# Moving the bulk weight loads of a fused adaLN, sliding-attention and MLP kernel to the GpSimd queue

## The chip, the cores and the metric

One core of one Trainium2 chip. The metric is the device time of one execution in microseconds (us); for the kernel before it is the median of 7 runs, 181.19 us (178.92 to 184.17). The profiled execution is one of these, at 178.92 us, and its span from first to last instruction is 177.2 us, so 1.7 us lie around the span. Sums are made inside the span.

## The reference

A transformer block with modulated layer norms: D = 448, 2048 tokens, 16 heads of 28, an attention in which each token sees 8 earlier tokens at a distance of 2, and an MLP with F = 1792. All tensors are bf16.

```
mod = silu(c) @ w_mod                      # six rows of 448: sa, ca, ga, sb, cb, gb
h = layernorm(x) * (1 + ca) + sa
q, k, v = split(h @ wqkv)                  # 16 heads of 28
o = softmax over the 8 keys at s, s-2, ..., s-14 (those >= 0) of (q . k) / sqrt(28), times v
x = x + ga * (o @ wo)
h = layernorm(x) * (1 + cb) + sb
x = x + gb * (gelu(layernorm(h) @ w1 + b1) @ w2 + b2)
```

## The kernel before

**Tiles and stages.** The tokens are split by parity into two sequences of 1024, so that a distance of 2 becomes a distance of 1, and into 16 blocks of 128 tokens. There are five kinds of work:

- the head: loads of x, of the first modulation columns (`wm_st`), of the Q, K, V weights; silu(c) and two groups of small matmuls give the scale and shift columns `mod_col`;
- `front_ln` and `front_qk` for chunks of 2, 2, 4, 4 and 4 blocks: statistics (L505, L506), 1/std, normalized rows z (L528), a transpose into hT, then the matmuls `pq` (Q and K, L585 and L591) and `pv` (V). The first 8 blocks are transposed on TensorE (L639); the other 8 by DMA transposes (L657) with scale and shift applied afterwards on VectorE (L661). V rows are cast into `vstage` and stored to the HBM scratch `v_hbm` (L719);
- `attention(b)`, nine of them: V windows loaded back from `v_hbm` into `vb` (L782), scores `lt` (L796), exponentials (L806), mask (L814), denominators `pd` (L828), products `po` (L836), division into `oT` (L862);
- `out_proj(t)`, 16 of them: `pw` (L877), residual (L881), the second and third layer norm with 1/std on GpSimd (L523), rows y (L528), a DMA transpose into yT (L903), the residual with bias `x1p` on GpSimd (L907);
- `mlp(j)`, four tiles of 512 tokens: w1 matmuls (`p<-yT,w_s`, L585 and L591), gelu (L937), w2 matmuls (`p<-w_s,hm`, L950), sum (L958), store.

Three phases follow each other: attention 0 to 4 and MLP tile 0; attention 5 and 6 and tile 1; attention 7 and 8 and tiles 2 and 3. The work up to the first w1 matmul is here called the front part.

**What sets the order.** Each piece is a task with an engine, an assumed time and the keys that it reads and writes. A list scheduler (`Planner.forward`, L148) simulates the engines with these assumed times, tries 300 orders by changing ranks (`plan`, L243), and emits every engine's instructions in the order of the best one. Engines run in that order and wait by semaphores alone. An entry of `order_after` places a task in the planned order, but makes no semaphore wait.

**Queues.** In the kernel before every DMA but one is issued from SyncE, in order: the head loads, then (marked `free`, so that the planner may place them anywhere) the second modulation weights `wmod2`, `wo_s`, x blocks 8 to 15, the biases, `w1_s`, `w2_s`, and between them the V stores (L719), the V window loads (L782), the transposes and the outputs. Each DMA takes the next of 8 completion semaphores, and waits until the DMA eight before it has landed. `mods()` (L724) makes four broadcast modulation rows: matmul `pb` (L731), a cast on ScalarE, a store to `mod_hbm` (L738), a broadcast load `mod_bc` (L740), with which `wo_s` (L743) and `w2_s` (L758) are scaled on VectorE.

**Weights of Q and K.** They land in `wqk_st` in two halves of the contraction rows each (`wq` a and b, `wk` a and b). `spread` (L666, instruction L675) copies them so that a head of 28 takes 32 columns: one copy for each half of the rows, four in all. In VectorE's order the four are q a, k a, q b, k b. Every `pq` of Q needs both q copies.

Of the kernel before, what the change touches and what calls it, by code (L numbers as in the profile page):

```python
# [11 lines left out]
FP32 = mybir.dt.float32  # L12
# [5 lines left out]
DP = 512  # L18
KT = 4
KOFF = (0, 128, 192, 320)  # L20
HP = 32
FT = F // 128
# [25 lines left out]
DMA_RATE = 330e3  # L48
SWITCH, SAME = 0.095, 1.0
SEM = 0.07  # L50
DRAIN = {"PE": 0.165, "DVE": 0.085, "ACT": 0.105, "POOL": 0.05, "SP": 0.0}
# [27 lines left out]
class Planner:  # L79
# [68 lines left out]
    def forward(self):  # L148
# [13 lines left out]
        while len(order) < len(self.tasks):  # L162
            started = False
            for e in ("PE", "DVE", "ACT", "POOL", "SP"):
# [4 lines left out]
                for t in ready[e]:  # L169
                    if ready_at[t] > now or (shared and t.port):  # L170
                        continue
                    key = (t.rank + (SAME if e == "PE" and t.mode_in == mode else 0.0), -t.n)
                    if best is not None and key < best_key:
                        continue
                    need = {}
                    for b in t.bufs:
                        if b.slot is None:
                            need[b.room] = need.get(b.room, 0) + 1
                    if all(sum(x <= now for x in room[r]) >= n for r, n in need.items()):
                        best, best_key = t, key  # L180
# [99 lines left out]
def kernel(  # L280
# [57 lines left out]
    mod_col = cst.tile([128, 2 * KT], FP32, name="mod_col")  # L338
    mod_half = cst.tile([128, 2 * KT], FP32, name="mod_half")
# [29 lines left out]
    chain_dma = []  # L369

    def load(fn, nbytes, writes, reads=(), bufs=(), free=False):
        t = add("SP", max(0.5, nbytes / DMA_RATE), fn, writes=writes, reads=reads, bufs=bufs, late=1.8,
                order_after=list(chain_dma))
        if not free:
            chain_dma[:] = [t]

    def load_k(dst, src, key, bufs=(), free=False):
        n = src.shape[1]
        for h in range(2):
            load(lambda h=h: nc.sync.dma_start(out=dst()[:, 2 * h:2 * h + 2],  # L380
                                               in_=src[KOFF[2 * h]:KOFF[2 * h] + 256].rearrange("(kt p) n -> p kt n", p=128)),
                 256 * n * 2, [key + "ab"[h]], bufs=bufs, free=free)

    def load_m(dst, col, key, bufs, free=False):
        src = w_mod[:, col:col + 2 * D]
        load(lambda: nc.sync.dma_start(out=dst()[:, 0:2], in_=src[0:256].rearrange("(kt p) n -> p kt n", p=128)),
             512 * D * 2, [key + "a"], bufs=bufs, free=free)
        load(lambda: nc.sync.dma_start(out=dst()[:, 3], in_=src[320:448]), 256 * D * 2, [key + "b"], bufs=bufs, free=free)
        load(lambda: nc.sync.dma_start(out=dst()[64:128, 2], in_=src[256:320]), 128 * D * 2, [key + "c"], bufs=bufs, free=free)

    def fill_m(dst, key, bufs, one, rank):

        def fn():
            nc.gpsimd.memset(dst()[0:64, 2], 0.0)
            if one is not None:
                nc.gpsimd.memset(dst()[0:1, 2, one:one + D], 1.0)

        add("POOL", 1.3, fn, writes=[key + "z"], bufs=bufs, rank_add=rank)

    def load_x(b0, b1):  # L400
        load(lambda: nc.sync.dma_start(out=x_all[:, b0:b1, :], in_=xv[b0 // 8, :, b0 % 8:(b1 - 1) % 8 + 1, :]),
             (b1 - b0) * 128 * D * 2, [f"x{b}" for b in range(b0, b1)], free=b0 >= 8)
# [3 lines left out]
    add("ACT", 0.4, lambda: nc.scalar.dma_start(out=c_row[:], in_=c), writes=["c_row"], late=1.6, rank_add=500)  # L406

    tbl0 = add("ACT", 1.28, lambda: nc.scalar.preload_act_table_set(EXP_SET), rank_add=400)
    load_x(0, 2)
    fill_m(lambda: wm_st.t[:], "wm", [wm_st], D, 850)  # L410
    load_m(lambda: wm_st.t[:], 0, "wm", [wm_st])
    load_k(lambda: wqk_st.t[:, 0], A_wqkv[:, 0:D + HP - DH], "wq", [wqk_st])
    load_k(lambda: wqk_st.t[:, 1], A_wqkv[:, D:2 * D + HP - DH], "wk", [wqk_st])
    load_x(2, 4)
    load_k(lambda: Wv[:], A_wqkv[:, 2 * D:3 * D], "wv")
    load_x(4, 8)
# [7 lines left out]
    load(v_pads, 3 * LEAD * DP * 2, ["v_pads"], reads=["warm_w"], free=True)  # L424
    for i in range(2):
        fill_m(lambda i=i: wmod2[i].t[:], f"wmod2{i}", [wmod2[i]], 0 if i == 1 else None, 300)
        load_m(lambda i=i: wmod2[i].t[:], (2 + 2 * i) * D, f"wmod2{i}", [wmod2[i]], free=True)
    add("POOL", 1.6, lambda: nc.gpsimd.memset(wo_s[:], 0.0), writes=["wo"], rank_add=440)
    wo_v = A_wo.rearrange("(ft r d) n -> r d ft n", r=4, d=DH)
    for r in range(4):  # L430
        load(lambda r=r: nc.sync.dma_start(out=wo_s[HP * r:HP * r + DH, :, :], in_=wo_v[r]), D * D // 2, [f"wo{r}"],
             reads=["wo"], free=True)
    for b in (8, 12):
        load_x(b, b + 4)
    b2_bc = sb("zh", [128, D], BF16, "b2_bc")
    load(lambda: nc.sync.dma_start(out=b2_bc.t[:], in_=B_b2.partition_broadcast(128)), 128 * D * 2, ["b2"], bufs=[b2_bc], free=True)
    load(lambda: nc.sync.dma_start(out=b1_rows[:], in_=B_b1.rearrange("(f p) -> f p", p=128)), F * 2, ["b1_rows"], free=True)
    for kt in range(KT):
        load(lambda kt=kt: nc.sync.dma_start(out=w1_s[:, kt], in_=B_w1[KOFF[kt]:KOFF[kt] + 128]), F * 256, [f"w1{kt}"], free=True)
    for i in range(4):  # L440
        f0, f1 = 4 * i, min(4 * i + 4, FT)
        load(lambda f0=f0, f1=f1: nc.sync.dma_start(
            out=w2_s[:, f0:f1], in_=B_w2[128 * f0:128 * f1].rearrange("(ft p) n -> p ft n", p=128)),
            (f1 - f0) * 256 * D, [f"w2l{f // 2}" for f in range(f0, f1, 2)], free=True)
# [8 lines left out]
    late_pool = []  # L453

    def pool_late():
        gate = add("POOL", 0.1, lambda: nc.gpsimd.memset(wqk_st.t[0:1, :, KT - 1, 0:8], 0.0), bufs=[wqk_st],
                   writes=["wqb", "wkb"])
        for us, fn, writes, reads, ra in late_pool:
            add("POOL", us, fn, writes=writes, reads=reads, rank_add=ra, order_after=[gate])

# [4 lines left out]
         ["ident"], gated=False, rank_add=800)  # L465
    pool(0.1, lambda: nc.gpsimd.memset(neg_half[:], -0.5), ["neg_half"])
# [72 lines left out]
    def c_cols():  # L539
        for kt in range(KT):  # L540
            nc.tensor.matmul(psc.t[:, kt:kt + 1], lhsT=c_row[0:1, KOFF[kt]:KOFF[kt] + 128], rhs=one1[:],
                             start=True, stop=True)

    P.wrote(add("PE", 0.2, c_cols, mode="32x128", reads=["c_row", "one1"], bufs=[psc]), psc)
    add("ACT", 0.15, lambda: nc.scalar.activation(out=e_c[:], in_=psc.t[:], func=ACT.Exp, scale=-1.0), bufs=[psc],
        writes=["e_c"], after=[tbl0])
    add("DVE", 0.08, lambda: nc.vector.tensor_copy(out=c_col[:], in_=psc.t[:]), bufs=[psc], writes=["c_col"])
    add("DVE", 0.08, lambda: nc.vector.tensor_scalar_add(out=e_c[:], in0=e_c[:], scalar1=1.0), writes=["e_c"])
    add("DVE", 0.1, lambda: nc.vector.reciprocal(out=e_c[:], in_=e_c[:]), writes=["e_c"])

    def silu():
        nc.vector.tensor_tensor(out=silu_bf[:], in0=e_c[:], in1=c_col[:], op=ALU.mult)
        nc.vector.memset(silu_bf[0:64, 2:3], 0.0)
        nc.vector.memset(silu_bf[0:1, 2:3], 1.0)

    add("DVE", 0.2, silu, reads=["e_c", "c_col"], writes=["silu"])
    pscol = ps_one([128, 2 * KT], "ps_col")

# [482 lines left out]
```

The softmax here doesn't subtract the row's maximum and nothing guards it: scores larger than these inputs give would overflow.

## Time and profile before

| | |
|---|---|
| median of 7 runs | 181.19 us |
| profiled execution, and its span | 178.92 us, 177.2 us |
| TensorE busy in the span | 165.5 us (93%) |
| VectorE, ScalarE, GpSimd busy | 117.0, 107.6, 49.9 us |
| first Q matmul; last `pw` before the MLP ends; first w1 matmul | 9.30; 67.78; 70.79 us |
| last w2 sum starts; end of span | 174.26; 177.2 us |
| bytes moved by DMA | 19.84 MB, nearly all on the queue of SyncE |
| one DMA issue on SyncE | 0.34 to 0.6 us; a DMA transpose 1.25 us |
| the one DMA issue on ScalarE (c) | 0.50 us |

TensorE appears as PE, its weight loads as PEld, VectorE as DVE, ScalarE as ACT, GpSimd as POOL, SyncE as SP; "SPq" is a queue's issue. A line number is that of the listing above. In the waits and the timelines, the engine after the arrow is the one whose work ended the wait.

### The profile page before, as it was taken

How to read it: one execution, taken by the hardware profiler on the slowest of the kernel's cores; microseconds unless marked ns; L12 is line 12 of the kernel's file. 1: busy time of each engine (PE TensorE's matmuls, PEld its weight loads, DVE VectorE, ACT ScalarE, POOL GpSimd, SP SyncE). 2: the span in 40 equal slices, each digit the busy share in tenths (PEclk: the TensorE clock that was granted, in tenths of full speed). 3: DMA queues.
4: the chain of work that ended last, by engine and by line, in shares of the span. 5: the costliest groups of instructions: out<-in, count | busy, mean ns of one | idle time of the engine just before them, and what ended most of it. 6: DMA issues, size and time to landing. Idle time of an engine off the chain costs nothing.

```text
span 177.2 us, 5017 instructions
## 1 busy us (share of the span) xinstructions
PE 165.5 (93%) x2067; PEld 79.9 (45%) x2085; DVE 117.0 (66%) x318; ACT 107.6 (61%) x195; POOL 49.9 (28%) x83
## 2 busy tenths in 40 slices
PE   7898999979999993999999999999999999999993
PEld 2554644444445431434555343555444354443562
DVE  2768995657999789999148459995589962010121
ACT  3347959887884977555838975825975520725200
POOL 8460022001125517754022036342053442000000
PEclk9999999999999999999999999999999999999999
DMA  5999945576997995201401600026100114001011
GB/s 167 321 357 308 281 122 120 147 170 111 318 268 192 321 141 144 66 2 28 95 4 34 191 0 4 1 58 117 55 4 0 31 30 111 0 4 52 0 52 52
DMA packets 28725, 19.84 MB, mean 112 GB/s; under 512 B 14465, under 2 KB 28062, under 8 KB 28702
## 3 DMA queue, kind: packets, MB, share of 16 engines
q1 hardware_dynamic: 28700, 19.52, 42.0%
q8 instruction: 16, 0.26, 0.6%
q14 instruction: 7, 0.06, 0.1%
q10 hardware_dynamic: 2, 0.00, 0.0%
HBM read 12.41 MB, written 3.96 MB: 92 GB/s over the span
## 4 chain that ended last, share of the span: by engine, by line
PE 74%; DMA 11%; DVE 4%; SPq 3%; ACT 3%; issue 2%; ACTq 0%
PE p L950 25%; PE p L585 21%; PE pw L877 6%; PE pq L585 6%; PE p L591 5%; DMA v_hbm<-vstage 4%; PE pv L585 3%; DMA x_all<-in_A_x_dram 3%; DMA yT<-y 2%; PE lt L796 2%; DMA vb<-v_hbm 2%; PE po L836 2%; DVE st_all L505 2%; PE pq L591 2%; SPq L380 1%
## 5 line engine op out<-in xcount | busy, mean ns | idle before, releaser
L937 ACT ACTIVATE hm<-p,b_col 128x512 bf16<-128x512 f32 x56 | 34.9, 687 | 30.1 <-PE p L585 16.1
L950 PE MATMUL p<-w_s,hm 128*128 128x448 bf16 (+1 forms) x238 | 44.8, 342 | 0.0
L585 PE MATMUL p<-yT,w_s 128*128 128x512 bf16 x160 | 38.7, 380 | 3.8 <-issue 3.5
L523 POOL TENSOR_TENSOR rs_all<-tv_all,neg_half 128x1 f32<-128x1 f32 (+1 forms) x34 | 22.6, 673 | 55.2 <-DVE tv_all L520 50.8
L950 PEld LDWEIGHTS <-hm 128*128 128x128 bf16 x238 | 22.4, 98 | 18.9 <-issue 0.9
L958 DVE TENSOR_TENSOR x_all<-p,x1p 128x448 bf16<-128x448 f32 (+1 forms) x17 | 10.1, 596 | 29.8 <-PE p L950 29.8
L907 POOL TENSOR_TENSOR x1p<-x_all,gbb_bc 128x448 f32<-128x448 bf16 x16 | 17.7, 1108 | 33.8 <-DVE x_all L958 12.9
L585 PEld LDWEIGHTS <-w_s 128*128 128x128 bf16 x168 | 15.2, 98 | 23.7 <-issue 7.8
L585 PE MATMUL pq<-hT,Wqk 128*128 128x512 bf16 (+1 forms) x111 | 23.0, 334 | 1.2 <-issue 0.6
L806 ACT ACTIVATE et<-lt 128x464 bf16<-128x464 f32 x36 | 17.3, 571 | 8.3 <-PE lt L796 8.2
L505 DVE BATCH_NORM_STATS2 st_all<-x_all 128x6 f32<-128x448 bf16 x32 | 19.0, 613 | 2.6 <-DMA x_all<-in_A_x_dram 2.5
L814 DVE TENSOR_TENSOR et<-et,mask 128x928 bf16<-128x928 bf16 x18 | 11.7, 667 | 6.0 <-ACT et L806 6.0
L528 DVE TENSOR_SCALAR z<-x_all,mv,rs_all 128x512 bf16<-128x512 bf16 (+1 forms) x32 | 13.0, 426 | 3.7 <-POOL rs_all L523 1.8
L585 PEld LDWEIGHTS <-Wqk 128*128 128x128 bf16 x120 | 10.4, 98 | 10.2 <-issue 2.5
L877 PE MATMUL pw<-wo_s,oT 128*128 128x448 bf16 x64 | 14.5, 354 | 0.3 <-DVE oT L862 0.2
L881 DVE TENSOR_TENSOR x_all<-pw,x_all 128x448 bf16<-128x448 f32 x16 | 9.9, 617 | 5.5 <-PE pw L877 5.5
L862 DVE TENSOR_TENSOR oT<-po,den 128x456 bf16<-128x456 f32 x18 | 10.7, 626 | 3.7 <-ACT den L852 3.7
L701 ACT CAST qT<-pq 128x512 bf16<-128x512 f32 (+1 forms) x20 | 9.3, 512 | 5.2 <-PE pq L591 3.2
L585 PE MATMUL pv<-Wv,hT 128*128 128x448 bf16 x48 | 10.4, 353 | 0.0
L715 ACT CAST vstage<-pv 128x448 bf16<-128x448 f32 x16 | 7.9, 554 | 4.2 <-PE pv L591 3.8
L701 ACT CAST kT<-pq 128x512 bf16<-128x512 f32 (+1 forms) x20 | 9.1, 512 | 2.1 <-PE pq L585 1.3
L849 ACT ACTIVATE den<-pd 128x464 f32<-128x464 f32 x18 | 9.2, 572 | 1.4 <-PE pd L828 1.4
(85 smaller groups left out, 172.4 us busy)
## 6 DMA issues: line engine op xcount, KB each, us to landing
w_s<-in_B_w_dram SPq DMA_DIRECT2D x7, 448.0 KB, 4.7
vb<-v_hbm SPq DMA_DIRECT2D x18, 128.0 KB, 2.8
v_hbm<-vstage SPq DMA_DIRECT2D x8, 256.0 KB
out_dram<-x_all SPq DMA_DIRECT2D x7, 224.0 KB, 3.0
x_all<-in_A_x_dram SPq DMA_DIRECT2D x3, 448.0 KB, 6.2
wqk_st<-in_A_wqkv_dram SPq DMA_DIRECT2D x4, 226.0 KB
wmod<-in_w_mod_dram SPq DMA_DIRECT2D x2, 448.0 KB
x_all<-in_A_x_dram SPq DMA_DIRECT2D x2, 224.0 KB
```

The costliest lines, as they stand in the source:

```text
L505: add("DVE", 0.53, lambda: nc.vector.bn_stats(out=st_all[:, sl, :], in_=src()), reads=key, writes=[f"st{sl}"])
L523: lambda: nc.gpsimd.tensor_tensor(out=rs_all[:, which, b0:b0 + n], in0=tv_all[:, which, b0:b0 + n], in1=neg_half[:, 0:n], op=ALU.pow),
L528: return add("DVE", us, lambda: nc.vector.tensor_scalar(out=dst(), in0=src(), scalar1=mv[:, b, 0:1], scalar2=rs_all[:, which, b:b + 1], op ...
L585: nc.tensor.matmul(outs[i].t[:], lhsT=w(i, kt, slice(0, 128)), rhs=x(i, kt, slice(0, 128)), start=(n == 0 and not last), stop=(n == 2 and ...
L591: nc.tensor.matmul(outs[i].t[:], lhsT=w(i, kt, rows), rhs=x(i, kt, rows), start=not last, stop=last, tile_position=(r0, 0))
L701: add("ACT", 0.06 + n / 1200, lambda dst=dst, p=pq[i]: nc.scalar.copy(out=dst, in_=p.t[:]), bufs=[pq[i]], writes=w)
L806: ex = add("ACT", 0.45, lambda r=r: nc.scalar.activation(out=et.t[:, r].rearrange("p n ft c -> p (n ft c)"), in_=lts[r].t[:].rearrange("p ...
L814: nc.vector.tensor_tensor(out=ev, in0=ev, in1=mask[:], op=ALU.mult)
L877: nc.tensor.matmul(pw.t[:], lhsT=oT[:, ft, c0:c0 + 128], rhs=wo_s[:, ft, :], start=(ft == 0), stop=(ft == 3))
L907: P.wrote(add("POOL", 1.05, lambda: nc.gpsimd.tensor_tensor(out=xp.t[:], in0=x_all[:, t, :], in1=gbb2_bc[:], op=ALU.add), reads=[f"x{t}", ...
L937: gl = add("ACT", 0.57, lambda f=f, p=p1[i]: nc.scalar.activation(out=hm_at(f), in_=p.t[:], func=ACT.Gelu_apprx_tanh, bias=b1_col[:, f:f + ...
L950: nc.tensor.matmul(p2.t[:], lhsT=hm_at(f)[:, bi * 128:(bi + 1) * 128], rhs=w2_s[:, f, c0:c1], start=(f == 0), stop=(f == FT - 1))
```

## The change

1. **Bulk loads go to GpSimd.** `wmod2` (4 DMAs), `wo_s` (4), x blocks 8 to 15 (2), b2 (1), `w1_s` (4) and `w2_s` (4) are issued from GpSimd's queue, in this order, after a gate that waits for the last copy of `spread`.
2. **Each is held back.** Ahead of each bulk DMA (of `wo_s` only the first) VectorE writes one element of its target; the DMA waits for that write. In the planner the write stands after the bulk load two before it; on the chip that is only a place in VectorE's order.
3. **Stores move.** The V rows and the modulation rows are stored from ScalarE's queue. SyncE keeps the head loads, V windows, `mod_bc`, transposes and outputs: 66 DMAs where it had 97.
4. **Q and K are spread by head halves**: a copy takes all rows of 8 heads, so it needs both halves of its weight, and a `pq` needs one copy. VectorE's order is q 0, q 1, k 0, k 1.
5. **The modulation weights** lie on 112 partitions of 4 rows each, loaded in two DMAs of 448 KB that need no zero fill; the constant 1 comes from an addend (`one_cb`, `tensor_scalar_add`) in place of a row of ones.
6. **The planner** knows a DMA bandwidth resource "BW" beside the issue time (0.8 us for a bulk DMA on GpSimd, 0.5 us on ScalarE).

```
-DMA_RATE = 330e3
+DMA_RATE, TR_BYTES = 340e3, 400e3
...
+    def bulk(fn, nbytes, writes, at, reads=(), bufs=()):
+        k = len(chain["bulk"])
+        if at is not None:
+            add("DVE", 0.06, lambda: nc.vector.memset(at(), 0.0), writes=[f"go{k}"], bufs=bufs, order_after=chain["bulk"][-2:-1])
+        t, u = dma("POOL", 0.8, fn, nbytes, writes, list(reads) + [f"go{k}"], bufs, chain["bulk_t"], 2.2)
+        chain["bulk_t"] = [t]
...
+    def load_m(go, eng, dst, col, key, bufs, gated):
+        src = w_mod[:, col:col + 2 * D].rearrange("(p kt) n -> p kt n", kt=KT)
+        for h in range(2):
+            at = [lambda h=h: dst()[0:1, 2 * h, 0:1]] if gated else []
+            go(lambda h=h: eng.dma_start(out=dst()[0:KC, 2 * h:2 * h + 2], in_=src[:, 2 * h:2 * h + 2]), 448 * D * 2, [key + "ab"[h]],
+               *at, bufs=bufs)
...
+    def bulk_loads():
+        for i in range(2):
+            load_m(bulk, nc.gpsimd, lambda i=i: wmod2[i].t[:], (2 + 2 * i) * D, f"wmod2{i}", [wmod2[i]], True)
+        wo_v = A_wo.rearrange("(ft r d) n -> r d ft n", r=4, d=DH)
+        for r in range(4):
+            bulk(lambda r=r: nc.gpsimd.dma_start(out=wo_s[HP * r:HP * r + DH, :, :], in_=wo_v[r]), D * D // 2, [f"wo{r}"],
+                 None if r else lambda: wo_s[0:1, 0, 0:1], reads=["wo"])
+        load_x(bulk, nc.gpsimd, 8, 12, True)
+        load_x(bulk, nc.gpsimd, 12, 16, True)
...
+        for kt in range(KT):
+            bulk(lambda kt=kt: nc.gpsimd.dma_start(out=w1_s[:, kt], in_=B_w1[KOFF[kt]:KOFF[kt] + 128]), F * 256, [f"w1{kt}"],
+                 lambda kt=kt: w1_s[0:1, kt, 0:1])
...
-        o = Wqk[:, 2 * h2:2 * h2 + 2, half]
+        o = Wqk[:, :, half, 8 * h2:8 * h2 + 8]
...
-            P.wrote(add("PE", pack_us(n), mm, mode=pack_mode(turn), reads=[f"W{half}0", f"W{half}1"] + hk, bufs=[hc] + pq), *pq)
+            P.wrote(add("PE", pack_us(n), mm, mode=pack_mode(turn), reads=[f"W{half}{mp % 2}"] + hk, bufs=[hc] + pq), *pq)
...
-            add("SP", 0.8, lambda r0=r0, vs=vs: nc.sync.dma_start(
+            dma("ACT", 0.5, lambda r0=r0, vs=vs: nc.scalar.dma_start(
...
-        add("SP", 0.5, lambda: nc.sync.dma_start(out=mod_hbm[:], in_=mod_rows.t[0:128:HP, :]), bufs=[mod_rows],
-            writes=["mod_hbm"], late=2.0)
+        dma("ACT", 0.5, lambda: nc.scalar.dma_start(out=mod_hbm[:], in_=mod_rows.t[0:128:HP, :]), 4 * D * 2, ["mod_hbm"], bufs=[mod_rows])
```

## The prediction

> **What bounds the kernel now.** I read the busy shares first (TensorE 93% of the span), then the chain of work that ended last, then busy time by stage, then the timelines of each engine around the largest gap of TensorE. Busy time by stage splits the span at the first Q matmul, the last `pw` before the MLP, the first w1 matmul and the last sum:
>
> ```profile
> core 0: us, PE busy (x) PEld busy (x) DVE busy (x) ACT busy (x) POOL busy (x), PEclk, DMA share, GB/s
> 9.30:67.78 58.48, 55.63 (x973) 28.04 (x980) 48.59 (x133) 46.60 (x100) 14.38 (x32) 1.00 0.84 218
> 67.78:70.79 3.01, 0.01 (x2) 0.03 (x1) 2.98 (x4) 2.05 (x2) 1.91 (x3) 1.00 0.49 112
> 70.79:174.26 103.47, 102.62 (x1034) 48.30 (x1042) 60.01 (x162) 55.94 (x88) 28.06 (x37) 1.00 0.17 42
> ```
>
> After 70.79 TensorE idles 0.85 us in 103: nothing can be won there. Before it, TensorE idles 2.85 us within the front part and 3.0 us at its end, and starts at 9.30. VectorE, with 48.59 of 58.48 us, is not far behind. The chain around the gap at 67.78:
>
> ```profile
> 57.87 6.23 DMA v_hbm<-vstage
> ...
> 64.17 0.63 SPq L782
> ...
> 64.86 0.59 SPq L782
> ...
> 65.54 4.13 DMA yT<-y
> 69.67 1.11 issue
> 70.79 0.38 PE p L585
> ```
>
> A V store of 256 KB takes 6.23 us because three w2 loads were issued just ahead of it on SyncE's one queue; the V window loads wait for it, and the transposes of y are behind them in SyncE's order. VectorE is the second arm of the same gap:
>
> ```profile
> 62.82 1.16 DVE L758 TENSOR_TENSOR w_s<-w_s,mod_bc 128x896 bf16<-128x896 bf16 x2 [1.76 <-DMA w_s<-in_B_w_dram]
> ...
> 64.98 0.41 DVE L528 TENSOR_SCALAR y<-h,mv,rs_all 128x512 bf16<-128x512 bf16 x1
> 65.30 4.75 DVE L758 TENSOR_TENSOR w_s<-w_s,mod_bc 128x896 bf16<-128x896 bf16 x4
> ```
>
> VectorE waits 1.76 us for a w2 load, then makes the last y of tile 0 at 64.98; from its end (65.39) to the first w1 matmul are 5.4 us. And the head:
>
> ```profile
> 8.21 0.42 DVE L675 COPY Wqk<-wqk_st 128x1024 bf16<-128x1024 bf16 x1
> 9.03 1.10 DVE L675 COPY Wqk<-wqk_st 128x1024 bf16<-128x1024 bf16 x3 [0.41 <-DMA wqk_st<-in_A_wqkv_dram]
> ```
>
> The first Q matmuls need the first and third of these copies (q a, q b); the second waits until 9.03 for k a. TensorE does one matmul at 9.30 and goes on at 9.85.
>
> **What the Trainium skill says.** DMA: Bandwidth & Descriptors, section Queues, rings and completion order: each DMA engine takes the rows that have work in turn, packet by packet. So a bulk load on GpSimd's row no longer stands wholly ahead of a V store. The trace agrees on the problem (6.23 us), not yet on the cure. The same page, section SWDGE vs HWDGE vs iDMA: descriptors of a DMA issued from GpSimd are written by GpSimd's own cores. No run here shows it; the trace has no such DMA. SBUF — State Buffer, section Who interferes with whom: a VectorE operation with two SBUF inputs and a GpSimd operation that reads SBUF exclude each other. The trace agrees: the L758 scaling takes 0.58 us each at 62.82 with GpSimd idle, and 1.19 each at 65.30 beside L747 and L907 on GpSimd.
>
> **The change, part by part.** I call p the time that one bulk DMA holds GpSimd, and T the start of the first w1 matmul (70.79 now). The matmuls before T, and those after it, are the same set, so the span moves as T does.
>
> *Head.* In the new order the first Q group needs one copy, q 0, which waits for q b. The q b load (226 KB) lands before k a, so about 226 KB / 323 GB/s = 0.7 us before 9.03, at 8.3. Plus a copy of 0.42 and 0.1 to hand over: first Q group at 8.8, where it effectively starts at 9.58 now (9.85 less the one matmul of 0.27 done early). TensorE could therefore reach T at 8.8 + 55.6 = 64.4 with no idle. The two GpSimd fills of wm_st and one head DMA of 0.5 us disappear; the bytes ahead of q b are the same, so I count nothing. The rows of x blocks 2 and 3 land near 10.3 as before; their z's no longer have statistics of blocks 4 to 7 between them, which hides there.
>
> *GpSimd up to x block 8.* The gate waits for the last copy, about 10.3. Then come 3.5 us of memsets and masks as in its timeline now (10.19 to 13.67) plus 0.2 for `one_cb`, and 9 DMAs up to and with x blocks 8 to 11 (4 wmod2, 4 wo_s, 1 x). So that load is issued by 10.3 + 3.7 + 9p = 14.0 + 9p. Landing takes about 3.0 us more: the 128 KB window loads take 2.8 from the start of an issue of 0.6, and 330 KB more at 330 GB/s add 1.0, less 0.2. The one-element write ahead of it stands in VectorE's order after the four z's of blocks 4 to 7, about 19.7 us; at p over 0.64 GpSimd gets there later, so it holds back nothing.
>
> *The price p.* SBUF — State Buffer, section A bandwidth-pool intuition that's wrong, states about 0.62 us for a GpSimd DMA alone and 3.1 us beside a VectorE copy; DMA: Bandwidth & Descriptors, section Latency and other measured facts, about 1 us to the first byte. The nearest row of the trace, an issue on SyncE, is 0.34 to 0.6. I take p = 0.8, as the planner of the diff does, between 0.62 and 1.0, as few long two-port copies run on VectorE from 10 to 22 us. Data of x block 8 then land at 17.0 + 7.2 = 24.2.
>
> *VectorE.* In the new order VectorE stands at the statistics of block 8 right after the two hT operations of blocks 4 to 7, about 21.9 us (16 transposes end at 8.8 + 12.3, plus two times 0.5, the first overlapping). So it waits 17.0 + 9p - 21.9 = 9p - 4.9, or 2.3 us; now these statistics run at 19.17 without a wait. From 9.30 to the end of the last y VectorE is busy 48.59 - 2.48 (the L758 after it) = 46.1 us now. Added: two more L758 ahead of that y, 1.16; 14 element writes of 0.06, 0.8. That makes 48.1. Its other idle pieces: 1.8 us before 22 us (0.18 + 1.0 + 0.61), kept; after it 7.8 in nine pieces, of which 1.76 (w2) goes, and of the other 6.0 I keep half, since an engine that comes later waits less. The last y ends at 9.3 + 48.1 + 1.8 + 3.0 + 2.3 = 64.5. If L758 met GpSimd at 1.19, 2.4 us more.
>
> *SyncE.* The transpose of y for block 2 is now issued well ahead of that for block 3, and no V store is ahead of either; issue to landing is 3.8 us for yT. With 0.1 to hand over T = 64.5 + 3.9 = 68.4, 2.4 us earlier than 70.79. TensorE's own bound of 64.4 leaves 4 us for its idle pieces (2.85 now), so VectorE decides, not TensorE.
>
> *ScalarE.* Nine stores at 0.50 (the row of c) are 4.5 us, and four stand right behind the cast that they wait for. Behind them are evacuations that TensorE waits for. 46.6 + 4.5 = 51.1 us in the 59.6 up to 68.4 is hidden; without cover, 4.5.
>
> *Later bulk loads.* w1's last piece is issued behind three `x1p` (1.1 each) and two powers, near 46 us; w2's near 48 to 55. They land some 3 to 4 us later, ahead of their use at 55 and 68: nothing, but a power queued behind a load comes p later and so does a y; with no cover 1 to 2 us.
>
> Sum: 177.2 - 2.4 = 174.8 for the span, 176.5 for that execution. The median stands 2.27 above the profiled execution, so 181.19 - 2.4 = 178.8.
>
> **Rivals.**
> *VectorE gives it back.* With p = 1.0 the wait at block 8 is 4.1 us, the last y ends at 66.3, T is 70.2 and the time 180.6; at p = 1.07 nothing is left. For it: VectorE's 83% busy share; against it: a late engine waits less elsewhere.
> *Slower: descriptors cost more.* Two-port copies and GpSimd's descriptor writing block each other, so p averages 1.5: x block 8 lands at 30.5, VectorE waits 8.6, T = 74.7, time 181.2 + 3.9 = 185.1. It is over 1% slower from p = 1.27. For it: the stated 3.1 us, and z, hT and weight copies on VectorE in that window; against it: statistics, most of the work there, are not copies.
> *The element writes do not hold anything back.* As worked out for x block 8, GpSimd itself is the pace. Then removing them changes nothing and the forecast stands: all that acts is the other queue.
> *TensorE-bound.* If p is 0.62 the load lands at 23.3 at the earliest (issue after the write at 19.7), T is 67.5, time 177.9; with VectorE's other waits gone too, T nears 66 and the time 176.4.
>
> **How the numbers follow.** About 1% (1.8 us) is what a measurement can tell from no change. Forecast and its faster neighbour (p under 0.85): 0.46, own range 176.3 to 179.3. Given back, within 1% either way: 0.26. Slower, by p, by port conflicts or by ScalarE's load: 0.28. The range 176 to 184 leaves out a fifth, most of it at the slow end. Predicted: 178.8.
>
> **What would show it.** Right: first Q group near 8.8; bulk DMAs on GpSimd of 0.8 us each; VectorE waiting some 2 us for x block 8 near 22 to 24; no V store over 4 us; the last y of tile 0 near 64.5 and the first w1 matmul near 68.4; the stretch after it 103 us long. Wrong: DMA rows on GpSimd over 1.2 us, TensorE waiting for hT of blocks 8 to 11 near 40 us, scores or casts late behind stores on ScalarE, or a stretch after T longer than 104 us.

## The result and the profile after

The kernel after the change takes 184.69 us in the median of 27 runs (180.71 to 188.73); the kernel before takes 181.68 us in 64 runs (178.73 to 187.41). The ratio is 1.010, 95% interval 1.0053 to 1.0147, formed from undisturbed runs alone, which lie at the low end of both spreads: slower by some 1%, where 1.3% faster was forecast. The profiled execution is one at 184.44 us, near the median of all runs, with a span of 182.7. It is 5.5 us over the profiled execution of before, three times what the ratio says, so the sizes read from it are those of a bad case.

The page of the kernel after, with one DMA queue (packets, MB, share of 16 engines), the chain by engine, and DMA issues (KB each, and median us from issue to landing):

```profile
q0 software_dynamic: 1664, 6.48, 14.1%
...
PE 77%; DMA 13%; ACT 3%; issue 2%; POOL 1%; DVE 1%; SPq 0%; POOLq 0%; DVEq 0%
...
v_hbm<-vstage ACTq DMA_DIRECT2D x8, 256.0 KB, 3.8
...
x_all<-in_A_x_dram POOLq DMA_DIRECT2D x2, 448.0 KB, 6.7
```

and, in the view of the DMAs alone, the transposes:

```profile
hT<-z SPq DMA_TRANSPOSE x8, 5.7
```

The new queue q0 carries 6.48 MB, and DMA has 13% of the chain where it had 11. The V stores land in 3.8 us, as hoped. But the transposes into hT take 5.7 us in the median of the five whose landing is on record (2.5 to 9.6), and the x loads take 6.7. Of the eight transposes of before only one landing is on record, 2.4 us; that one value is the measure of before in what follows. Busy time by stage, split at the first Q group, the last `po` before the largest gap of TensorE, the gap's end, the first w1 matmul and the last sum:

```profile
core 0: us, PE busy (x) PEld busy (x) DVE busy (x) ACT busy (x) POOL busy (x), PEclk, DMA share, GB/s
9.31:43.90 34.59, 32.22 (x655) 17.51 (x656) 24.69 (x73) 27.38 (x63) 17.34 (x39) 0.95 0.90 226
43.90:49.65 5.75, 0.20 (x25) 0.09 (x12) 1.44 (x5) 2.37 (x4) 0.00 (x0) 0.71 1.14 91
49.65:76.51 26.86, 26.32 (x321) 11.25 (x325) 26.70 (x78) 16.66 (x33) 13.46 (x18) 0.94 0.68 181
76.51:179.97 103.46, 102.34 (x1035) 48.12 (x1042) 57.62 (x159) 58.82 (x92) 24.75 (x34) 1.00 0.17 43
```

Read the second row: for 5.75 us TensorE does almost nothing and the other engines little. The DMA share is 1.14, that is, packets were under way on its engines all the time, and yet they move 91 GB/s. The last row is the stretch after T, 103.46 us, where before had 103.47. So all of the difference lies ahead of T, which went from 70.79 to 76.51. The chain of waits names what ended the gap:

```profile
24.00 5.13 DMA mod_hbm<-mod_rows
29.14 3.98 DMA mod_bc<-mod_hbm
...
33.26 1.19 POOL gbb_bc L780
...
36.58 1.33 POOL rs_all L546
...
38.14 9.97 DMA hT<-z
48.16 0.05 issue
48.21 1.39 DVE hT L692 x4
49.65 0.61 PE pq L609
```

The last transpose of blocks 8 to 11 is issued at 38.14 and lands 9.97 us later; VectorE scales, and the Q group starts. What else was on its way stands in the timeline of GpSimd:

```profile
16.92 2.45 POOL L456 DMA_DIRECT2D wo_s<-in_A_wo_dram  x4
20.54 1.54 POOL L414 DMA_DIRECT2D x_all<-in_A_x_dram  x2 [0.93 <-DVE x_all L385]
23.71 0.55 POOL L460 DMA_DIRECT2D b_bc<-in_B_b_dram  x1 [1.63 <-DVE w_s L385]
24.25 0.54 POOL L463 DMA_DIRECT2D w_s<-in_B_w_dram  x1
...
37.85 1.17 POOL L463 DMA_DIRECT2D w_s<-in_B_w_dram  x2
```

and in that of SyncE:

```profile
31.84 2.60 SPq L688 DMA_TRANSPOSE hT<-z  x2
34.54 0.59 SPq L815 DMA_DIRECT2D vb<-v_hbm  x1
35.22 2.23 SPq L688 DMA_TRANSPOSE hT<-z  x1
37.51 0.59 SPq L815 DMA_DIRECT2D vb<-v_hbm  x1
38.14 6.13 SPq L688 DMA_TRANSPOSE hT<-z  x4
```

At 37.85 and 38.48, one 0.3 us ahead of that transpose and one as much behind it, GpSimd issues the w1 loads of row groups 1 and 2, 917 KB together, which nobody needs before T. In the kernel before, the transposes of blocks 8 to 11 were issued from 25.67 to 30.92; now they come 6 to 7 us later (31.84 to 38.14), which has used up the other work of TensorE.

**My theory** after this: (A) the two w1 loads on their own queue share the DMA engines with the transposes and stretch the last one from 2.4 us to 10; TensorE stands still, and its matmuls run at half rate for a while after. **Rival B**: x lands late and SyncE issues four transposes and two window loads one by one; the w1 loads don't matter. **Rival C**: the element writes are the loss.

### The profile page after: what moved, and what is told of

Read it like the earlier page. It is cut to its first block, busy times and chain, and to the rows that moved or that the text cites. A ratio compares the mean times of both kernels' runs of the same rounds, so it can differ in the third digit from the quotient of the medians.

```text
span 182.7 us, 5045 instructions
## 1 busy us (share of the span) xinstructions
PE 168.1 (92%) x2068; PEld 80.4 (44%) x2082; DVE 114.9 (63%) x333; ACT 108.2 (59%) x195; POOL 57.8 (32%) x99
## 3 DMA queue, kind: packets, MB, share of 16 engines
q0 software_dynamic: 1664, 6.48, 14.1%
## 4 chain that ended last, share of the span: by engine, by line
PE 77%; DMA 13%; ACT 3%; issue 2%; POOL 1%; DVE 1%; SPq 0%; POOLq 0%; DVEq 0%
PE p L982 24%; PE p L609 20%; PE pq L609 9%; PE pw L910 6%; DMA hT<-z 5%; PE p L615 5%; PE pv L609 4%; DMA wm_st<-in_w_mod_dram 3%; DMA mod_hbm<-mod_rows 3%; PE pq L615 2%; DMA mod_bc<-mod_hbm 2%; PE po L869 2%; PE lt L829 2%; ACT hT L683 1%; PE pd L861 1%
## 5 line engine op out<-in xcount | busy, mean ns | idle before, releaser
L609 PE MATMUL p<-yT,w_s 128*128 128x512 bf16 x160 | 38.4, 380 | 0.7 <-issue 0.5
L940 POOL TENSOR_TENSOR x1p<-x_all,gbb_bc 128x448 f32<-128x448 bf16 x16 | 17.0, 1067 | 51.4 <-DVE x_all L914 24.8
L546 POOL TENSOR_TENSOR rs_all<-tv_all,neg_half 128x1 f32<-128x1 f32 (+1 forms) x34 | 21.5, 649 | 30.9 <-DVE tv_all L543 30.6
L609 PE MATMUL pq<-hT,Wqk 128*128 128x512 bf16 (+1 forms) x115 | 24.0, 347 | 6.3 <-DVE hT L692 5.6
L609 PEld LDWEIGHTS <-w_s 128*128 128x128 bf16 x168 | 15.1, 97 | 20.7 <-issue 4.6
L839 ACT ACTIVATE et<-lt 128x464 bf16<-128x464 f32 x36 | 17.4, 564 | 10.4 <-PE lt L829 10.2
L609 PEld LDWEIGHTS <-Wqk 128*128 128x128 bf16 x120 | 10.8, 100 | 16.7 <-DVE hT L692 5.7
L551 DVE TENSOR_SCALAR z<-x_all,mv,rs_all 128x512 bf16<-128x512 bf16 (+1 forms) x32 | 12.5, 418 | 3.7 <-POOL rs_all L546 2.2
L910 PE MATMUL pw<-wo_s,oT 128*128 128x448 bf16 x64 | 13.8, 353 | 0.0
L609 PE MATMUL pv<-Wv,hT 128*128 128x448 bf16 x48 | 11.6, 382 | 0.0
```

The costliest lines, as they stand in the source:

```text
L546: lambda: nc.gpsimd.tensor_tensor(out=rs_all[:, which, b0:b0 + n], in0=tv_all[:, which, b0:b0 + n], in1=neg_half[:, 0:n], op=ALU.pow),
L551: return add("DVE", us, lambda: nc.vector.tensor_scalar(out=dst(), in0=src(), scalar1=mv[:, b, 0:1], scalar2=rs_all[:, which, b:b + 1], op ...
L609: nc.tensor.matmul(outs[i].t[:], lhsT=w(i, kt, slice(0, 128)), rhs=x(i, kt, slice(0, 128)), start=(n == 0 and not last), stop=(n == 2 and ...
L839: ex = add("ACT", 0.45, lambda r=r: nc.scalar.activation(out=et.t[:, r].rearrange("p n ft c -> p (n ft c)"), in_=lts[r].t[:].rearrange("p ...
L910: nc.tensor.matmul(pw.t[:], lhsT=oT[:, ft, c0:c0 + 128], rhs=wo_s[:, ft, :], start=(ft == 0), stop=(ft == 3))
L940: P.wrote(add("POOL", 1.05, lambda: nc.gpsimd.tensor_tensor(out=xp.t[:], in0=x_all[:, t, :], in1=gbb2_bc[:], op=ALU.add), reads=[f"x{t}", ...
```

## The experiments

Fifteen kernels ran in four groups, each group on one chip beside runs of the kernel before, whose medians were 182.78, 181.75, 182.13 and 181.44 us. In the experiments' listings lines stand a little further down: L620 is L609, L699 is L688, L703 is L692, L425 is L414. `move` puts bulk loads (numbered in the order of `bulk_loads`, 12 and 13 being w1 groups 1 and 2), with their element writes, at another place of the finished order; everything else keeps its order. "First Q" is the start of the first Q group (of before, as in the prediction, without the one matmul done early), "gap" TensorE's wait for hT of blocks 8 to 11, T the first w1 matmul, each from the one profiled execution. The ratio to before stands with its 95% interval where one was formed.

| kernel | median us | ratio to before | first Q | gap | T |
|---|---|---|---|---|---|
| before (profiled at 178.92) | 181.68 | 1 | 9.58 | 0 | 70.8 |
| after (profiled at 184.44) | 184.69 | 1.010 (1.005 to 1.015) | 9.31 | 5.55 | 76.5 |
| c_after | 187.08 | not given | 10.40 | 6.97 | 79.4 |
| e1_w1_later | 180.23 | not given | 11.54 | 0 | 73.0 |
| e2_no_writes | 182.52 | not given | 11.40 | 0.31 | 73.6 |
| e3_x_first | 182.34 | not given | 10.09 | 3.33 | 75.5 |
| e5_two_fills | 180.13 | 0.989 (0.984 to 0.993) | 9.45 | 0 | 70.5 |
| e6_w1_sync | 180.92 | 0.989 (0.979 to 0.999) | 10.95 | 0.35 | 73.4 |
| e7_stores_sync | 183.96 | 1.017 (1.010 to 1.024) | 10.18 | 0 | 74.4 |
| e8_wm_rows | 179.63 | 0.984 (0.975 to 0.993) | 11.17 | 0 | 72.1 |
| e9_fill_stall | 184.84 | not given | 11.08 | 0.89 | 78.4 |
| e10_best | 180.26 | 0.990 (0.987 to 0.994) | 10.01 | 0 | 70.7 |
| e11_after | 182.80 | 1.011 (0.997 to 1.024) | 9.05 | 2.49 | 72.7 |
| e12_w1_later | 180.22 | 0.999 (0.995 to 1.002) | 11.78 | 0 | 71.9 |
| e13_wm_128 | 178.80 | 0.987 (0.976 to 0.997) | 10.75 | 0 | 71.5 |
| e14_wm_three | 179.82 | 0.982 (0.970 to 0.994) | 9.00 | 0 | 70.5 |
| e15_one_w1 | 181.30 | 1.000 (0.995 to 1.004) | 11.10 | 3.50 | 75.7 |

**c_after**: the changed kernel, unaltered.

> The changed kernel as it is, beside the variants of this call. Theory A (the two w1 loads that GpSimd issues at 38 us share the DMA engines with the transposes of z for blocks 8 to 11): the last transpose that the hT of blocks 8 to 11 needs takes about 10 us from issue to landing, TensorE stands about 5.5 us before the first matmul on that chunk, the first w1 matmul is at 75 to 76.5 us, and the time is about 1% over the kernel before. Theory B (the chunk is late because x blocks 8 to 11 landed late and SyncE then issues four transposes and two window loads one after the other): the same stand, but with a transpose of 3 to 4 us once an execution without a lowered clock is profiled.

187.08 us (186.83 to 187.41), the upper end of its spread and more than expected; T came at 79.4, not at 75 to 76.5. The timeline of TensorE:

```profile
44.08 0.80 PE L869 MATMUL po<-et,vb 64*32 64x57 bf16 x64
51.85 2.74 PE L609 MATMUL pq<-hT,Wqk 128*128 128x512 bf16 x6 [6.97 <-DVE hT L692]
54.52 0.61 PE L615 MATMUL pq<-hT,Wqk 64*128 64x512 bf16 x2
```

The gap is 6.97 us here, and the six matmuls behind it take 2.74 us, 0.46 each.

**e1_w1_later**: the two w1 loads behind the last scaling of hT of blocks 8 to 11.

```
     P.plan()
+    move([12, 13], scaled[8])
     P.emit()
```

> The order of the changed kernel, with only the w1 loads of row groups 1 and 2 and their element writes moved behind the scale and shift of hT for blocks 8 to 11. Theory A: the slow transpose falls from 10 us to 3 to 5 us, the 5.5 us stand of TensorE falls under 1.5 us, and the time falls by 4 to 5 us against the changed kernel, to 1 to 2% under the kernel before. Theory B: transpose and stand change by less than 1 us and so does the time.

180.23 us (179.39 to 180.98), 6.9 under c_after on the same chip where reading A had said 4 to 5, and no gap. The same kernel was run again in the third group, beside the unaltered change:

**e12_w1_later** and **e11_after**.

> The kernel of e1_w1_later again. Theory (the w1 loads against the transposes are the loss): 4 to 7 us under e11_after and 1 to 1.5% under before, no gap of TensorE over 1.5 us ahead of the first w1 matmul. Rival (the first time was a lucky chip): less than 2 us under e11_after.

> The changed kernel again, unaltered, as the measure for the other three on this chip: between 184 and 187.5, TensorE's gap ahead of the Q group of blocks 8 to 11 between 4 and 7 us.

180.22 (178.60 to 181.73, 18 runs) against 182.80 (180.59 to 184.95, 4 runs): 2.6 lower, not the 4 to 7 expected, because this time the gap of the unaltered change was 2.49 us and not 7. Against the kernel before the ratio is 0.999: moving the two loads takes the loss away, but the 1 to 1.5% of gain that was expected is not there. The timeline of TensorE in e12_w1_later:

```profile
44.30 0.76 PE L881 MATMUL po<-et,vb 64*32 64x57 bf16 x64
45.06 1.46 PE L620 MATMUL pq<-hT,Wqk 128*128 128x512 bf16 x6
46.45 0.39 PE L626 MATMUL pq<-hT,Wqk 64*128 64x512 bf16 x2
```

and of its VectorE, which did not wait for the transpose issued at 40.07:

```profile
43.52 1.39 DVE L703 TENSOR_SCALAR hT<-hT,mod_col 128x512 bf16<-128x512 bf16 x4
```

The transpose had thus landed within 3.5 us, and the same six matmuls take 1.46 us. In e11_after it took 7.20 us, in the profile of the result 9.97, in c_after 10.44: one program, three sizes of the same gap. The chains of waits of e11_after and, below it, of c_after:

```profile
37.30 7.20 DMA hT<-z
```

```profile
39.87 10.44 DMA hT<-z
```

A is supported: the w1 loads make the gap, which is 0 in all eight kernels that issue both of them later. They do it only because the transposes are late as well: in e12_w1_later the scaling ends at 44.9 and TensorE runs out of other work at 45.06, so nothing was to spare. Nor has the collision as such gone: the moved loads, issued at 44.88, meet the transpose issued at 44.10, which lands after 7.30 us, but TensorE never waits for that one.

**e15_one_w1**: half of the bytes.

```
+    move([13], scaled[8])
```

> The changed kernel with one of the two w1 loads (row group 1, 459 KB) left in the way of the transposes and the other moved behind the scaling of hT of blocks 8 to 11. If the harm grows with the bytes, that transpose lands after 5 to 8 us, TensorE waits 0 to 2.5 us, and the time lies between the two: 180.5 to 183. If any bulk load on the other ring does the same harm, the landing is 7 to 10.5 us and the time 183 to 187 as in the unaltered change.

The chain of waits has

```profile
39.83 7.58 DMA hT<-z
```

and the gap is 3.50, more than expected, in an execution at 183.61; but the median is 181.30 (179.16 to 185.73), as expected for a harm that grows with the bytes, and the ratio to before, 1.000, is that of e12_w1_later. One load left in the way thus costs nothing that the times show. The landing is in the range that was named for a harm that grows with the bytes, but also in that of the other reading, and e11_after with all the bytes reached 7.20. I take the time as in favour of bytes, no more.

**e6_w1_sync**: the same two loads issued from SyncE, ahead of the transpose of block 11, which in SyncE's order is the second of the four and not, as I had thought, the last.

```
-            bulk(lambda kt=kt: nc.gpsimd.dma_start(out=w1_s[:, kt], in_=B_w1[KOFF[kt]:KOFF[kt] + 128]), F * 256, [f"w1{kt}"],
+            bulk(lambda kt=kt: (nc.sync if kt in (1, 2) else nc.gpsimd).dma_start(out=w1_s[:, kt], in_=B_w1[KOFF[kt]:KOFF[kt] + 128]), F * 256, [f"w1{kt}"],
...
+    move([12, 13], trs[11], before=True)
```

> The two colliding w1 loads (917 KB) are issued from SyncE, right ahead of the transpose of z for block 11, instead of from GpSimd; nothing else moves. Theory (two rings share the engines, packet against packet): in one queue that transpose waits for the 917 KB, about 2.9 us at 320 GB/s, and takes its own 2.4; issue to landing near 5 to 6 us instead of 10, TensorE idle near 1 to 3 us instead of 5.6 to 7.0, the time 2 to 5 us under the 187.1 of the changed kernel in the call before. Rival (the bytes ahead decide, whichever queue they are in): landing near 10 us, TensorE idle 5 us or more, the time unchanged.

SyncE's timeline and, below it, the chain of waits:

```profile
35.75 0.85 SPq L474 DMA_DIRECT2D w_s<-in_B_w_dram  x2
36.65 1.19 SPq L699 DMA_TRANSPOSE hT<-z  x1
```

```profile
36.65 5.83 DMA hT<-z
```

The transpose behind 917 KB in one queue lands after 5.83 us; I had worked out 2.9 + 2.4 = 5.3. The gap is 0.35 us, and the time is 180.92. The same bytes on GpSimd's queue cost up to 10.44. So it is not only the bytes ahead. That two queues at once are worse for the transpose than one queue in order is the nearest reading, but this run changes more than their number: the loads come ahead of the second transpose and not the last, and leave GpSimd's queue, which the page of the profile calls software, for SyncE's, which it calls hardware. No run has them on a second queue of the same kind. The Trainium skill, DMA: Bandwidth & Descriptors, section Queues, rings and completion order, says that an engine takes its queues in turn, a packet at a time; if that were all, the transpose could lose no more than these bytes take, 2.9 us. The runs show up to 8 us lost.

The traces narrow it down. In the result, c_after, e3_x_first, e11_after and e15_one_w1 the transpose lands 0.1 to 0.4 us behind the last of these loads, and the loads are slow as well: the later one takes 9.3 us in the result. Of the 128 packets that carry the two loads there, half took under 0.29 us, but 19 over 1 us and one 4.73; the packets of the transposes, 256 bytes each, took 18 ns in the median, as in the kernel before. So a few packets stand for long while most go at their usual pace. What these wait for is open.

**e2_no_writes**: the element writes left out (14 of 0.06 us on VectorE); the order is kept.

```
+    for go, _ in bulks:
+        for g in go:
+            g.fn = lambda: None
```

> The changed kernel's order without the one-element writes, so that GpSimd's own order alone paces the bulk loads. As forecast (writes hold nothing that matters): x blocks 8 to 11 are issued at most 1 us earlier, the time changes by less than 1 us. If the writes hold back what they should: loads of x, b2 and the first w1 rows come 1 to 2.5 us earlier, so window loads and the store of the modulation rows take longer, and the time rises by 1 to 3 us; if they hold back what is late, the data of block 8 come 1 us earlier and the time falls by about 1 us.

182.52 us, 4.6 under c_after, which none of the readings had said. With the writes GpSimd waits 0.99, 1.25 and 1.63 us at `wmod`, x and b2; without them it issues x at 20.16 and VectorE starts on block 8 without a wait, as its timeline shows:

```profile
25.52 1.15 DVE L539 BATCH_NORM_STATS2 st_all<-x_all 128x6 f32<-128x448 bf16 x2
```

In c_after this was at 28.55, after a wait of 3.18, with the first Q group 1.0 us earlier. So the writes do hold the loads back, by 3 us for x. But this is no case for rival C by itself: the gap shrank to 0.31 while the w1 loads came at 39.99, 1.6 us behind the last transpose (38.41), and a new wait took its place:

```profile
PE po L881 <- DMA vb<-v_hbm: 2.4, 1, 2.4
```

A window load, issued at 23.40, took 8.58 us to land; that this is because nothing held the bulk loads apart any more is likely, but not shown.

**e3_x_first**: the loads of x blocks 8 to 15 ahead of those of `wo_s`.

```
+    move([8, 9], bulks[4][0][0], before=True)
```

> The changed kernel's order, with the loads of x blocks 8 to 15 ahead of the four wo_s loads on GpSimd, and their element writes moved likewise. Theory B: the data of block 8 land 3 us earlier, VectorE's wait of 3.5 us for them goes, the hT of blocks 8 to 11 comes 3 us earlier and TensorE's stand falls from 5.5 to 2.5 us; time 2.5 to 3 us less than the changed kernel. Theory A: the statistics come earlier, and the transposes are then issued before the w1 loads, so some of the stand goes too, but the transpose that meets the w1 loads still takes over 6 us; time 0 to 2 us less.

182.34 us, 4.7 under c_after; the gap is 3.33, not gone. VectorE no longer waits for x, and yet the last transpose is issued at 38.93, only 0.9 earlier than in c_after, since the power on GpSimd ahead of z now waits behind the bias row, whose wait for `mod_bc` grew to 6.81 us. B accounts for part of the lateness, not for the gap. But the fall of 4.7 us is more than either reading gave, and as the gap of the unaltered change alone varies from 2.49 to 6.97, one profile does not say how much of it is x.

**e7_stores_sync**: e1_w1_later with the nine stores back on SyncE.

```
-            dma("ACT", 0.5, lambda r0=r0, vs=vs: nc.scalar.dma_start(
+            dma("ACT", 0.5, lambda r0=r0, vs=vs: nc.sync.dma_start(
...
```

> The w1 loads as in e1_w1_later, and the eight V stores and the store of the modulation rows issued from SyncE again. Theory: the stores are hidden either way, or go back into SyncE's order ahead of window loads and transposes; the time is 0 to 3 us above the 180.2 of e1_w1_later, with transposes landing sooner than 5.9 us as one ring less has work. Rival (stores on the ACT queue are part of the loss): the time falls below 179.5.

183.96 us (182.28 to 184.79), a ratio of 1.017 where the other three of this group, which keep the stores on ScalarE's queue, have 0.984 to 0.989. TensorE waits 3.51 us at 59.93 for the hT of the last blocks, whose transpose, issued at 52.63 just behind two window loads that had stood 5.6 us behind a V store, took 5.84. The loss, 3.7 us over e1_w1_later, is a little more than expected. So in this order, which was planned with the stores on ScalarE, that part of the change is worth keeping; an order planned for SyncE was not tried.

**e5_two_fills**: e1_w1_later with two filler matmuls instead of six ahead of the first Q group. (Fillers, `pwm`, are matmuls of zeros that the planner puts where it expects TensorE idle.)

```
+    P.order = [(t, min(f, 2) if t.start > 8.0 else f) for t, f in P.order]
```

> The w1 loads stay where the run e1_w1_later put them; of the six filler matmuls ahead of the first Q group only two are left. Theory: TensorE is busy with fillers at half rate (0.43 us each) while hT and Wqk are ready about 1.5 us before it gets to them, so the first Q group comes near 10.0 instead of 11.5 and the first w1 matmul near 71.5 to 72 instead of 73.0; time 178.5 to 179.5. Rival: fewer fillers leave the clock at half for longer, the first Q groups take 0.2 us a matmul instead of 0.11, and nothing is won: the time stays at 180.2 or is above it.

First Q at 9.45, T at 70.5 as expected or better; the time is 180.13 (177.53 to 181.10), the same median as e1_w1_later. The profile, of an execution at 178.62, shows the gain, the median doesn't, and the ratios (0.989 against 0.999 for e12_w1_later) come from two chips: not settled.

**e8_wm_rows**, **e14_wm_three**, **e13_wm_128**: how the first modulation weights `wm_st` are loaded; all with the w1 loads later. e8 has another assignment of rows to partitions, e14 three pieces instead of two, e13 the three pieces and 128 partitions of the kernel before.

```
-        src = w_mod[:, col:col + 2 * D].rearrange("(p kt) n -> p kt n", kt=KT)
+        src = w_mod[:, col:col + 2 * D].rearrange("(kt p) n -> p kt n", kt=KT)
...
```

```
+        nc.sync.dma_start(out=wm_st.t[0:KC, 2], in_=wsrc[:, 2])
+        nc.sync.dma_start(out=wm_st.t[0:KC, 3], in_=wsrc[:, 3])
...
```

```
+        nc.sync.dma_start(out=wm_st.t[:, 3], in_=wsrc[320:448])
+        nc.sync.dma_start(out=wm_st.t[64:128, 2], in_=wsrc[256:320])
...
```

> The w1 loads as in e1_w1_later; the modulation weights are still loaded in two pieces to 112 partitions, but partition p takes rows p, 112 + p, 224 + p and 336 + p of them instead of four neighbouring rows. If the order of the rows makes the load slower than before, the second piece lands at 6.5 instead of 6.9 to 7.7, the first Q group starts near 10.0 and the time is 1 to 1.5 us under 180.2. If it is the 112 partitions or the two pieces, the landing stays near 7.3 and the time at 180.2.

> The w1 loads as in e12_w1_later; the second 392 KB piece of the first modulation weights is loaded as two of 196 KB, still to 112 partitions. If the number of pieces matters, the second modulation group starts near 6.5 and the time is 0.5 to 1.5 us under 180.2; if the 112 partitions or neither, it starts at 7.2 or later and the time stays at 180.2.

> The w1 loads as in e12_w1_later; the first modulation weights are loaded as in the kernel before (three pieces to 128 partitions, 784 KB), and silu(c) is also made in that layout (six more small operations on VectorE and ScalarE, all ahead of the landing). If the 112 partitions delay the landing, the second modulation group starts near 6.5 instead of 7.7 to 8.2, the first Q group near 9.5 to 10.5, and the time is 0.5 to 1.5 us under 180.2. If the rest of the head does (Q and K loads issued 0.6 us earlier on the same queue), it still starts at 7.2 or later and the time is that of e12_w1_later.

(A piece has 392 KB, as these texts say; the 448 KB of "The change" are too many.) The second modulation group starts at 7.71 (e8), 6.88 (e14) and 7.01 (e13, there not held by the load). In the thirteen other profiles of the two-piece form, the unaltered change among them, it starts at 6.89 to 8.15, and in the kernel before at 6.47. So nothing speaks for the order of the rows, and both three-piece forms are at the early end, with 128 partitions and with 112. That points to the number of pieces, no more: it is one profile each, and e11_after has 6.89 with two. e14's first Q at 9.00 and T at 70.5 are the best of the runs, and its ratio of 0.982 (0.970 to 0.994) is the lowest; with four runs, it is not shown to be better than the others with the w1 loads later.

**e10_best**: w1 later, x first and two fillers together.

> The three edits that helped, together: the two w1 loads later, the x loads of blocks 8 to 15 ahead of wo_s, and two fillers instead of six in the head. If they add up: first Q group near 9.5, x of blocks 8 to 11 about 2 us earlier, first w1 matmul near 69 to 70.5, time 177.5 to 179, some 2% under before. If x was not what the middle waited for once the transposes land in time, it equals e5_two_fills, about 1.1% under before.

180.26 us, ratio 0.990 (0.987 to 0.994): faster than both kernels by a little, but the edits do not add up, and it equals e5_two_fills as the second reading said: x is there without a wait, and T is 70.7 where e5_two_fills has 70.5. A wait of 1.5 us for yT has come at 126 us, in the MLP.

**e9_fill_stall**: the unaltered change with sixteen fillers in the gap.

```
+            for k in range(16):
+                nc.tensor.matmul(p.t[:], lhsT=warm_w[:, 0:128], rhs=warm_w[:], start=True, stop=True)
...
```

> The changed kernel with sixteen matmuls of no use (128x512, some 0.22 us each at full rate, 3.5 us in all) on TensorE right ahead of the Q group of blocks 8 to 11, that is, in the gap in which it waits for the transpose. Theory (the gap costs twice: once as idle time, and once more because the matmuls after it run at half rate for some 5 us): the gap stays, but the Q groups behind it take 0.22 us a matmul instead of 0.43, and where the gap is 5 us or more the time falls by 1.5 to 2.5 us against e11_after. Rival (the slow matmuls come from a limit that has nothing to do with the gap): the Q groups stay at half rate and the time is that of e11_after, or above it by what the fillers overrun the gap.

The times, 184.84 us (180.57 to 186.35) against 182.80 (180.59 to 184.95) for e11_after, overlap and decide nothing. The profile, of the execution at 186.35, does not meet the theory, as busy time in steps of 2 us shows:

```profile
48.00:50.00 2.00, 1.38 (x7) 1.00 1.98 153
50.00:52.00 2.00, 0.61 (x3) 1.00 0.64 90
52.00:54.00 2.00, 2.00 (x7) 0.58 0.40 80
54.00:56.00 2.00, 2.00 (x8) 0.57 0.74 161
```

The columns are length, TensorE busy, granted clock, DMA share and GB/s. The fillers end at 49.4; two short waits of 0.89 and 1.12 us remained, and the clock fell all the same, only later. That fits the rival; with two waits left in the gap it does not decide between the two.

## Why the prediction was wrong

**The step that failed** is "Later bulk loads": w1 and w2 "land some 3 to 4 us later, ahead of their use at 55 and 68: nothing". I asked of each load only when it lands and who needs it, and not what else is under way while it runs; and of w1 I placed only the last piece, near 46 us. Two of the w1 loads, issued from 37.85 on, cost TensorE 5.55 us in the profile of the result, without being late themselves. The prediction's own list of what would show it wrong has the very mark ("TensorE waiting for hT of blocks 8 to 11 near 40 us"), with no rival that gave it a cause or a price. That taking these loads out of the way removes the gap is shown, twice beside the unaltered change; why they hurt more than their bytes is not. Without the collision the kernel only equals the one before (0.999), so the gain that was forecast failed by further terms, which follow.

**A cost that no step had**: behind the gap TensorE is slow. In c_after, in steps of 2 us (columns as above):

```profile
48.00:50.00 2.00, 0.00 (x0) 0.99 1.17 170
50.00:52.00 2.00, 0.15 (x1) 0.50 1.72 182
52.00:54.00 2.00, 2.00 (x6) 0.50 0.43 79
54.00:56.00 2.00, 2.00 (x7) 0.50 0.51 128
```

The Trainium skill, TensorE: Matmul & The Clock Gate, section Part 1: The HAM clock gate, says that the array falls to half rate after an idle window of about 3.4 us and comes back after about as long a busy one. The traces agree on the two rates (0.50 and 1.00) and on how long the slow stretch lasts: 45.89 to 49.30 in e11_after, twice that in the profile of the result (46.30 to 53.12), where the gap ended at 49.65. They do not agree on the idle time ahead of it: in e11_after a gap of 2.49 us was enough and in e10_best one of 1.36, while the gap of 3.0 us in the kernel before was followed by a clock of 1.00. In steps of 2 us, e11_after and, below it, e10_best:

```profile
46.00:48.00 2.00, 1.97 (x5) 0.50 0.58 163
```

```profile
42.00:44.00 2.00, 2.00 (x68) 0.50 0.90 210
```

Behind the gap of e11_after six Q matmuls take 2.74 us instead of 1.46. In the profile of the result the matmuls from 49.65 to 54.4 are busy for 0.61 + 1.91 + 0.60 + 1.58 = 4.70 us, the same ones in e12_w1_later for 1.46 + 0.39 + 1.47 = 3.32. e9 did not show that filling the gap avoids it. And the profile of the result has one more such stretch, from 36.05 to 39.47, with no wait over 0.82 us ahead of it, in which six V matmuls take 2.42 us and not the 1.31 of e12_w1_later. So the length of a gap alone does not decide the clock, and that this gap made the matmuls behind it slow is not shown.

**The landing of x** was a size: "about 3.0 us more" after the end of its issue (forecast 21.2, measured 20.54 + 0.77 = 21.3) were 5.5; data at 26.85 instead of 24.2, and VectorE waited 3.46 us instead of 2.3. I had taken the rate of the queue with the engines to itself; they were 90% busy in that stage.

**The price p** was right: 2.45 / 4 = 0.61 for `wo_s`, 0.77 for x, 0.54 to 0.62 for w1, at the low end of 0.62 to 1.0 or a little under. The rival that made descriptors dear had the sign of the result, by a mechanism that the trace does not show: luck.

**"The element writes hold nothing back"** was wrong: GpSimd waits for them 1 to 1.6 us at a time, and x comes 3 us earlier without them (e2_no_writes). The sum set the write (19.7) against the end of the issue of x, 14.0 + 9p; its start, 14.0 + 8p, is past 19.7 only from p = 0.71 on. With `wo_s` at 0.61 GpSimd stood there at 19.6, and the write came at 20.16.

**The head** gave 0.3 us of the 0.8 forecast in the profile of the result: first Q at 9.31, forecast 8.8, and 9.0 to 11.8 over all runs. What decides there is not the copy of Q's weights. The second modulation group waits for `wm_st`, which I had counted at nothing ("the bytes ahead of q b are the same"), and behind it stand six fillers in TensorE's order, 1.46 us at full rate (e14_wm_three) and up to 2.77 at half (e1_w1_later).

**T and VectorE**: the gap of 3.0 us at T has gone, as forecast; the end of the last y was forecast at 64.5 and came at 72.95, behind the loss above. Without the collision it is 68.66 in e12_w1_later, and TensorE comes to T without a wait, at 71.88, so that there TensorE and not VectorE decides. Even with no collision and the good head of e14_wm_three, T is 70.5 and not 68.4: TensorE is busy for 57.6 us from the first Q to T where I had taken 55.6 from the trace of before. Some 1.2 of these 2.0 us are the clock, at which no step looked: e14_wm_three has a stretch at 0.50 too, from 36.35 to 39.77, while e12_w1_later, at 1.00 from its first Q to T, is busy for 56.4. The other 0.8 is open.

**ScalarE** and the **V stores** were right in the main: the nine stores ahead of T take 3.6 us to issue (0.36 to 0.57 each), beside 46.4 us of busy time from the first Q to T, which does not count them. The V stores land in 3.8 us in the median, though one took 4.7, over the mark of 4; e7_stores_sync shows that in this order taking this part back loses.

The account of T in the profile of the result, from 70.79: head -0.3, gap +5.55, slow matmuls behind it +1.4, the slow stretch at 36 us +1.2 (by the measure of the 57.6 above), gap at T -3.0, makes 75.6 of 76.5; the other 0.9 is spread over small pieces and stays unplaced. The slow stretch at 36 us lies ahead of the gap: without it TensorE would have waited that much longer there.

## What to carry to other kernels

When a load leaves a queue in which it stood in order, ask of it not only when it must land but what is under way when it starts: here a bulk load that nobody needed yet, set off within 0.3 us of a small transfer that the busiest engine was to wait for, was dearer than a late one (1.2% between the ratios of e11_after and e12_w1_later). Hold such loads back behind the consumer of the transfer that they would meet, and not behind a write that marks only that GpSimd may go on. And look at how much work covers that wait: here the same collision was dear because the transposes had become 6 to 7 us later and nothing was left for TensorE to do.

## What the runs showed of the hardware

- A DMA transpose of 128 x 512 bf16 landed in 2.4 us in the kernel before (the one of eight into hT with a landing on record), within 3.5 in e12_w1_later with the two w1 loads out of its way, in 5.8 behind 917 KB in its own queue (e6_w1_sync), and in 7.2 (e11_after) to 10.4 us (c_after) with these 917 KB on GpSimd's queue, 0.1 to 0.4 us behind the landing of the last of them.
- With transposes and bulk loads together the engines showed a share of 1.14 while they moved 91 GB/s (43.90 to 49.65 in the result); in its head, from 8 to 10 us, they moved 358 GB/s at a share of 1.10.
- TensorE ran at a clock of 0.50 for 3.4 us behind a gap of 2.49 us (e11_after) and one of 1.36 (e10_best), and in the result from 36.05 to 39.47 with no wait over 0.82 ahead of it; behind a gap of 3.0 us the kernel before stayed at 1.00.
- A plain DMA issued from GpSimd held it for 0.54 to 0.84 us in the result, also where VectorE was at work beside it.
